# Top-k attention and a gated feed-forward on one core: every step taken from one written list

## The chip, the cores and the metric

The kernel runs on one core of a Trainium2 chip. The metric is the device time of one execution in microseconds (us). The engines of the core work side by side, each through its own queue in order: TensorE (PE, with its weight loads PEld), VectorE (DVE), ScalarE (ACT), GpSimd (POOL), and SyncE (SP), which here issues most DMAs. TensorE writes to PSUM, eight banks of 512 f32 words for each of 128 partitions.

## The reference

Eight batches of eight heads, 576 positions, head width 64; then a feed-forward over 4608 tokens of width 512 with 2048 hidden columns. Its weights come as 64-bit floats.

```python
scores = scale * np.matmul(q, k.transpose(0, 1, 3, 2))
kth = np.partition(scores, -top_k, axis=-1)[..., -top_k:-top_k + 1]   # top_k = 32
scores = np.where(scores >= kth, scores, -1000000000.0)
attn = np.exp(scores - np.max(scores, axis=-1, keepdims=True))
attn = attn / (np.sum(attn, axis=-1, keepdims=True) + 1e-09)
x = heads_side_by_side(np.matmul(attn, v))       # (4608, 512)
h = x @ w_in                                     # w_in (512, 2048)
out = (h * np.cos(h)) @ w_out                    # w_out (2048, 512)
```

## The kernel before

The 4608 tokens are 36 blocks of 128 rows. A *unit* is one block and one pair of heads: 144 units, four to a block; unit n belongs to block n // 4. Each unit goes through these steps:

- `scores`: TensorE multiplies queries by keys into a PSUM tile `sc` (448 columns for each head; two such tiles exist) and into the shared banks `rim` (the last 128). Two units' scores can thus wait at most.
- `take_scores`: ACT copies them to `s` (four buffers).
- `fold_high`, `fold_sum`, `fold_low`: the 576 columns are folded to 288 larger and 288 smaller ones. VectorE makes the larger half (L267, reads `sc` and `s`), POOL the smaller; for units 8 to 10 (`BUSY`) VectorE makes both, the second with `fold_now` (L275). When the last fold that reads `sc` is done, that score tile is free for another unit.
- the search: VectorE finds the 32 largest in rounds of MAX8 and MATCH_REPLACE8: four on the larger halves, two on the smaller.
- `merge_first`, `merge_second`, `distances`, then `mask` and `exponentials` on ACT, `sums` and `reciprocal` on VectorE.
- for units 0 to 3, `turn`: TensorE transposes the probabilities. For all others `split` on POOL (two copies), `write_halves` and `transposes`: two DMAs on SP's queue, out to DRAM and back transposed into `ring` (five places).
- `values`: TensorE multiplies four units' probabilities by v, into `rim`; `take_values`: VectorE scales them into `xT`, the block's input of the feed-forward.

The feed-forward of a block: eight pieces of the first product (`ff1`, here F1.block.piece), two to a PSUM bank `mm` (two banks); `take_first` on ACT empties a bank after every second piece; `reduce_first`, `reduce_second`, `gate` on POOL and `sines` on ACT work on two halves; eight pieces of the second product (`ff2`, here F2.block.piece) gather in one `mm` bank; `take_second` and a DMA bring it out. F2 pieces 0 to 3 need the first gated half, 4 to 7 the second.

The weights arrive as 32 chunks of 512 64-bit columns in staging buffers: `decode_first` (ACT, two instructions), `decode_second` (VectorE, a shift, L151) and `decode_third` (POOL, an addition, L160). Chunks 0 to 15 are `w_in`, 16 to 31 `w_out`.

The order is made by rules: `slot(i, ...)` writes unit i's search and, around it, the later steps of units i-1 and i-2 and the scores of the next one or two units; `feed` puts pieces of F1 and F2 in, by a plan of four slots (`plan`), when `can_first` and `can_second` allow it by counts of ticks; the weight loads go to SP's queue in the first six slots, then to ACT's. Each engine carries out its own share in exactly that order.

Of the kernel before, what the change touches and what calls it, by code (L numbers as in the profile page):

```python
# [30 lines left out]
def kernel(  # L31
# [63 lines left out]
    BUSY = range(8, 11)  # L95
    ff = {"live": 0, "tick": 0, "now": 0, "end": False, "kind": 0, "half": 0, "open": 0, "late": False}

    wq = {"next": 0, "loaded": deque(), "second": deque(), "third": deque(), "done": 0, "ready": 0}

    def staged(spare=0):  # L100
        return sum(c[2] == spare for k in ("loaded", "second", "third") for c in wq[k])

    def load_weights(n, queue):
        for _ in range(n):
            i = wq["next"]
            if i >= len(chunks):
                return
            src, dst = chunks[i]
            if not DECODE:
                queue.dma_start(out=dst[0][:, dst[1]], in_=src)  # L110
                wq["next"] = wq["done"] = i + 1
                continue
            spare = i < 2 * NC + 10 and i % 2 == 1 and staged(1) < XB
            if spare:
                st = ffw.tile([P, CW, 2], I32, tag="x", name="st", bufs=XB)
            elif staged() + ff["live"] >= CHUNKS:
                return
            else:
                st = ffw.tile([P, CW, 2], I32, tag="g", name="st", bufs=CHUNKS)
            queue.dma_start(out=st.rearrange("p w i -> p (w i)"), in_=src)  # L120
            wq["loaded"].append((st, dst, int(spare)))
            wq["next"] = i + 1

# [3 lines left out]
    def decode_first(n):  # L127


        for _ in range(min(n, len(wq["loaded"]))):  # L130
            st, w, spare = wq["loaded"].popleft()
            lo, hi = st[:, :, 0], st[:, :, 1]
            nc.scalar.activation(
                out=w[0][:, w[1]], in_=hi.bitcast(F32), func=AF.Prelu, scale=2.0**-111, alpha=2.0**32
            )
            nc.scalar.mul(out=lo, in_=lo.bitcast(U32), mul=2.0**-29)
            wq["second"].append((st, w, spare))

    def decode_second(n):

        left = min(n, len(wq["second"]))
        while left:
            st, (w, c), spare = wq["second"].popleft()
            wq["third"].append((st, (w, c), spare))
            m = 1
            if left > 1 and wq["second"][0][1][0] is w:
                wq["third"].append(wq["second"].popleft())
                m = 2
            left -= m
            wi = w[:, c : c + m].bitcast(I32)  # L150
            nc.vector.tensor_scalar(  # L151
                out=wi, in0=wi, scalar1=3, scalar2=None, op0=ALU.logical_shift_left
            )

    def decode_third():

        while wq["third"]:
            st, w, _ = wq["third"].pop()
            wi = w[0][:, w[1]].bitcast(I32)
            nc.gpsimd.tensor_tensor(out=wi, in0=wi, in1=st[:, :, 0], op=ALU.add)  # L160
            wq["done"] += 1

# [69 lines left out]
    def scores(u):  # L235
        sc = u["sc"] = ps.tile([P, 2, 512], F32, tag="sc", name="sc", bufs=2)
        for to, k0, k1 in ((sc, 0, SB), (sc_ends[u["n"] % 2], SB, S)):
            for b, q0, rows, r0 in u["parts"]:
                for j in range(2):
                    d = slice(j * D, (j + 1) * D)  # L240
                    st = pairs[b, u["hp"]]
                    nc.tensor.matmul(  # L242
                        to[r0 : r0 + rows, rim_bank(r0, j) if k0 else place(u["hp"], j), 0 : k1 - k0],
                        st["q"][d, q0 : q0 + rows],
                        st["k"][d, k0:k1],
                        start=True,
                        stop=True,
                    )
# [61 lines left out]
    def topk_first(u, w):  # L310

        u["top"] = tops[u["n"] % len(tops)]
        if w:
            merge_first(w)
        if u["n"] not in BUSY:
            fold_sum(u)
        fold_high(u)
        if w:
            merge_second(w)
        if u["n"] in BUSY:  # L320
            fold_now(u)
        topk_round(u, 0, [lambda: distances(w), lambda: None] if w else ())

    def topk_round(u, rnd, between=(), ahead=None):
# [3 lines left out]
        search(  # L328
            at, rest[:, :, HS:S] if rnd == 0 else rest[:, :, 0:HS], rest[:, :, 0:HS], rnd < lasts,
            between if rnd < lasts else (),  # L330
        )
        if rnd < lasts:
            return
        del u["rest"]
        low = u.pop("low")
        for k in range(TOPK // 16):
            more = k < TOPK // 16 - 1
            if ahead and not more:
                ahead()
            search(top[:, :, 1 + 8 * k : 9 + 8 * k, 1], low, low, more, () if more else between)  # L340
# [560 lines left out]
```

## Time and profile before

| what | us |
| --- | --- |
| median of 3 runs | 1412.41 |
| lowest and highest run | 1411.02, 1412.88 |
| time of the profiled execution | 1412.72 |
| span of its trace | 1410.6 |
| granted TensorE clock over the span | 0.975 |

The span runs from the first instruction of the program in the trace to the last; what lies around it is not in the trace. In the page, a line of a group gives the source line, engine, operation, what is written from what, the count, then the busy time and the mean of one in ns, then the idle time of the engine just before them and what ended it. A line of the timeline gives start, duration, engine, line, operation and, in brackets, the wait ahead of it. A line of stretches gives from:to and length, then busy us (and instructions) of PE, PEld, DVE, ACT and POOL, then the granted TensorE clock, the DMA share and GB/s. A line of waits gives the total, how often, and the longest one. TensorE carries out each f32 matmul of the source as two instructions.

### The profile page before, as it was taken

The numbers are of one execution on the slowest core, as the hardware profiler recorded it, in microseconds if no ns is written. First come the engines' busy times: TensorE is split into PE (matmuls) and PEld (weight loads), VectorE is DVE, ScalarE is ACT, GpSimd is POOL, SyncE is SP. The second block draws the span as 40 slices with busy tenths as digits, with TensorE's granted clock in tenths as the row PEclk, the third lists the DMA queues.
The fourth block names the chain that finished last, engine by engine and source line by source line (L and its number), as shares of the span: only waits on it lengthen the run. The fifth ranks groups of instructions, "written<-read, shape, count | busy, mean of one in ns | idle before, by whom it ended". The sixth has DMA issues, their size and how long they took to land.

```text
span 1410.6 us, 32284 instructions
## 1 busy us (share of the span) xinstructions
PE 1354.6 (96%) x11264; PEld 977.2 (69%) x11264; DVE 1336.9 (95%) x5004; ACT 1140.9 (81%) x2043; POOL 1165.3 (83%) x804
## 2 busy tenths in 40 slices
PE   5558999999999999999999999999999999999998
PEld 3445777777777777777777777777777777777775
DVE  7999999999999999999999999999999999999931
ACT  7887888888888888888888888888888888888831
POOL 4778988888888888888888888888888888898810
PEclk6788999999999999999999999999999999999999
DMA  9566776867675576668666576666766566655540
GB/s 291 193 196 181 204 178 169 203 172 196 162 177 152 161 199 159 181 160 197 174 170 159 152 181 187 170 170 160 207 165 165 158 174 166 148 157 146 152 101 15
DMA packets 427442, 240.12 MB, mean 170 GB/s; under 512 B 375952, under 2 KB 392592, under 8 KB 427280
## 3 DMA queue, kind: packets, MB, share of 16 engines
q1 hardware_dynamic: 420720, 224.22, 61.3%
q10 hardware_dynamic: 6560, 13.85, 2.8%
q8 instruction: 88, 1.44, 0.4%
q14 instruction: 74, 0.61, 0.1%
HBM read 45.09 MB, written 101.19 MB: 104 GB/s over the span
## 4 chain that ended last, share of the span: by engine, by line
PE 91%; DVE 7%; ACT 1%; DMA 0%; POOL 0%; issue 0%; SPq 0%; POOLq 0%
PE o L628 36%; PE mm L553 35%; PE rim L475 10%; PE sc L242 8%; DVE top L359 3%; PE rim L242 2%; DVE rest L364 2%; DVE low L364 1%; DVE rest L267 1%; DVE w_out L151 0%; DVE w_in L151 0%; DMA st<-in_moe_w_in_dram 0%; PE warm L844 0%; DVE low L275 0%; ACT s L387 0%; ACT s L378 0%
## 5 line engine op out<-in xcount | busy, mean ns | idle before, releaser
L553 PEld LDWEIGHTS mm<-xT,w_in 128*128 128x128 f32 x4608 | 537.9, 192 | 70.4 <-issue 65.5
L553 PE MATMUL mm<-xT,w_in 128*128 128x128 f32 x4608 | 539.2, 275 | 2.4 <-DVE xT L491 1.7
L628 PE MATMUL o<-w_out,g 128*128 128x512 f32 x1152 | 524.7, 599 | 0.0
L359 DVE MAX8 top<-rest 128x8 f32<-128x288 f32 x1152 | 479.0, 451 | 0.0
L364 DVE MATCH_REPLACE8 rest<-top,rest 128x288 f32<-128x288 f32 x864 | 376.7, 444 | 0.0
L628 PEld LDWEIGHTS o<-w_out,g 128*128 128x128 f32 x1152 | 207.7, 190 | 219.5 <-issue 214.8
L410 POOL COPY halves<-s 128x2304 uint16<-128x2304 uint16 x140 | 294.9, 2107 | 43.3 <-ACT s L387 40.1
L378 ACT ACTIVATE s<-s,top 128x576 f32<-128x576 f32 x288 | 207.6, 768 | 111.1 <-DVE top L352 99.0
L359 DVE MAX8 top<-low 128x8 f32<-128x288 f32 x576 | 241.8, 449 | 0.4 <-POOL low L292 0.4
L387 ACT ACTIVATE s<-s,nd 128x576 f32<-128x576 f32 x288 | 220.4, 769 | 1.1
L292 POOL TENSOR_TENSOR low<-low,rest 128x576 int32<-128x576 int32 x141 | 199.3, 1413 | 11.0
L283 POOL TENSOR_TENSOR low<-s 128x576 int32<-128x576 int32 x141 | 199.6, 1415 | 6.4 <-ACT s L259 6.4
L598 POOL TENSOR_TENSOR x<-g,x 128x1024 f32<-128x1024 f32 x68 | 161.2, 2370 | 5.7
L242 PE MATMUL sc<-k,q 64*64 64x448 f32 (+1 forms) x1120 | 145.6, 564 | 16.2 <-DVE low L275 9.8
L615 POOL TENSOR_TENSOR g<-g,x 128x1024 f32<-128x1024 f32 x68 | 161.0, 2367 | 0.0
L257 ACT COPY s<-rim 64x256 f32<-64x256 f32 (+1 forms) x280 | 103.1, 368 | 61.6 <-PE rim L475 60.0
L475 PE MATMUL rim<-ring,v 128*64 128x128 f32 (+1 forms) x2560 | 139.0, 268 | 0.0
L475 PEld LDWEIGHTS rim<-ring,v 128*64 128x64 f32 x2560 | 130.0, 139 | 6.5 <-issue 5.7
L253 ACT COPY s<-sc 128x896 f32<-128x896 f32 (+1 forms) x144 | 128.4, 892 | 3.3 <-PE sc L242 3.2
L567 ACT ACTIVATE g<-mm 128x512 f32<-128x512 f32 x144 | 85.2, 592 | 56.5 <-PE mm L553 55.5
L364 DVE MATCH_REPLACE8 low<-top,low 128x288 f32<-128x288 f32 x288 | 125.4, 443 | 0.0
L267 DVE TENSOR_TENSOR rest<-sc,s 128x576 f32<-128x576 f32 x144 | 107.7, 748 | 7.1 <-ACT s L259 6.6
(55 smaller groups left out, 1155.7 us busy)
## 6 DMA issues: line engine op xcount, KB each, us to landing
rows<-halves SPq DMA_DIRECT2D x140, 640.0 KB, 3.5
out_dram<-ob ACTq DMA_DIRECT2D x36, 256.0 KB, 2.1
q<-in_q_dram SPq DMA_DIRECT2D x31, 288.0 KB, 4.4
st<-in_moe_w_in_dram SPq DMA_DIRECT2D x16, 512.0 KB, 5.8
v<-in_v_dram SPq DMA_DIRECT2D x32, 256.0 KB, 4.2
k<-in_k_dram SPq DMA_DIRECT2D x31, 144.0 KB, 4.2
k<-in_k_dram SPq DMA_DIRECT2D x32, 128.0 KB, 4.5
st<-in_moe_w_out_dram SPq DMA_DIRECT2D x8, 512.0 KB, 5.1
```

Of the source, the lines that this page charges most:

```text
L242: nc.tensor.matmul(to[r0 : r0 + rows, rim_bank(r0, j) if k0 else place(u["hp"], j), 0 : k1 - k0], st["q"][d, q0 : q0 + rows], st["k"][d, k ...
L283: nc.gpsimd.tensor_tensor(out=u["low"].bitcast(I32), in0=s[:, :, 0:HS], in1=s[:, :, HS:S], op=ALU.add)
L292: nc.gpsimd.tensor_tensor(out=low, in0=low, in1=u["rest"][:, :, HS:S].bitcast(I32), op=ALU.subtract)
L359: nc.vector.max(to[:, j], src[:, j])
L364: nc.vector.match_replace(rest[:, j], to[:, j], src[:, j], NEG)
L378: nc.scalar.activation(out=s[:, j], in_=s[:, j], func=AF.Prelu, bias=less[:, j], scale=1.0, alpha=FAR)
L387: nc.scalar.activation(out=s[:, j], in_=s[:, j], func=AF.Exp, bias=nd[:, j : j + 1], scale=SCALE, accum_out=den[:, j, 0:1],)
L410: nc.gpsimd.tensor_copy(out=halves[:, :, 0 : 2 * S], in_=s.rearrange("p (k h) -> p h k", h=2))
L475: nc.tensor.matmul(to[d, r], lhsT, rhs, start=(bank, j) not in begun, stop=c == NT - 1 and u in us[-2:] and r0 + rows == P,)
L553: nc.tensor.matmul(mm[:, at : at + w], w_in[f // FC][:, c, (f % FC) * P : (f % FC + 1) * P], blk["xT"][:, c], start=c == 0, stop=c == NC - 1,)
L598: nc.gpsimd.tensor_tensor(out=x, in0=g, in1=x, op=ALU.subtract)
L628: nc.tensor.matmul(o, g[:, at : at + P], w_out[f], start=f == 0, stop=f == NF - 1)
```

## The change

The rules (`slot`, `send`, `forward`, `drain`, `feed`, `feed_any`, `can_first`, `can_second`, the queues of pending work) are gone. One list names all steps in order, each by a short name with its unit or block, and a table `steps` maps names to functions; a loop at the end runs them. An engine still carries out its share in the order of the list. Some functions are cut up so that their parts can be listed apart: `scores` into Sa (448 columns) and Sb (the last 128), `turn` into T1, T2, T3 and their copies, `split` into sp1 and sp2, the first search round into R0 (MAX8) and R0m (MATCH_REPLACE8).

What the order does by engine, beside the new names:

- TensorE: the scores of unit 4 stand ahead of unit 0's transposes, those of 8 and 7 ahead of F1.0.0, and so on; from unit 15 on the even unit of a pair comes before the odd one (16, 15, 18, 17, ...), often with F pieces between. F1.0.6 and F1.0.7 come before the scores of unit 10; F2.0.0, F2.0.1 and the values of units 4 to 7 before the scores of unit 12. Ahead of the values of units 8 to 11, 12 to 15 and 16 to 19 there are two more F2 pieces than before, ahead of the next two values one more; from the values of units 28 to 31 on the counts are those of before, and from those of units 132 to 135 on again one to four F2 pieces more.
- VectorE: the shifts of the decode are single ones (before: two chunks in one where they were neighbours) in other places; `take_values` comes after the last MAX8 of a unit in place of before it.
- ACT: single decodes stand between masks, exponentials and score copies; the multiplication of `nd` goes from `mask` to `exponentials`.
- POOL: the same steps with the decode's additions spread.
- SP: all weight loads, those of chunks 24 to 31 too; chunks 0 to 2 are issued before unit 1's queries and keys.

The core of the diff:

```diff
+    def load_weights(k, kind):
+        src, dst = chunks[k]
...
+        nc.sync.dma_start(out=st.rearrange("p w i -> p (w i)"), in_=src)
+        staged[k] = st
...
+    def decode_second(k):
+        w, c = chunks[k][1]
+        wi = w[:, c].bitcast(I32)
+        eng = nc.gpsimd if k in SHIFT_BY_POOL else nc.vector
+        eng.tensor_scalar(
+            out=wi, in0=wi, scalar1=3, scalar2=None, op0=ALU.logical_shift_left
+        )
...
-    def scores(u):
-        sc = u["sc"] = ps.tile([P, 2, 512], F32, tag="sc", name="sc", bufs=2)
-        for to, k0, k1 in ((sc, 0, SB), (sc_ends[u["n"] % 2], SB, S)):
...
+    def scores(u, part):
+        if part == 0:
+            u["sc"] = ps.tile([P, 2, 512], F32, tag="sc", name="sc", bufs=2)
+        to, k0, k1 = ((u["sc"], 0, SB), (sc_ends[u["n"] % 2], SB, S))[part]
...
+    def largest(to, src):
+        late = list(between)
+        between.clear()
         for j in range(2):
             nc.vector.max(to[:, j], src[:, j])
-            if between:
-                between[j]()
...
+            n = (len(late) + 1) // 2
+            for f in late[n * j : n * (j + 1)]:
+                f()
...
-    for i in range(NU):
-        ff["now"] += 1
-        wq["ready"] = wq["done"]
-        u, w, x = (units[i - n] if n <= i else None for n in range(3))
-        z = valued.get(i)
-        slot(i, u, w, x, z)
...
+    for step, *of in order:
+        steps[step](*of)
```

`LOW_BY_POOL` and `SHIFT_BY_POOL` are empty lists, so no decode step changes its engine. `between` holds `distances`, `sums` and `reciprocal` of the unit before until the next MAX8 pair (C in the list puts the last two there).

The list for units 2 and 3 and for units 7 to 16 (Q: load queries and keys; VV: load v; L: load a chunk; D1, D2, D3: decode; K: `take_scores`; P0: merge and folds of VectorE; P0b: `fold_now`; fs, fl: POOL's folds; M: mask; E: exponentials; wr, tr: write and transpose; V, X: `values`, `take_values`; B1, B2: `take_first`, `take_second`; A0, A, N, G: the two reductions, sine and gate):

```
... P0.2 fs.2 L.14.g R0.2 T3e.0 Sa.3 M.1 R0m.2 fl.2 R1.2 Sb.3
D1.7 D1.8 R2.2 E.1 D2.8 R3.2 D3.8 Q0.2 D1.9 T1.1 D1.10 D2.9 T2.1 D2.6 D2.7 K.3 C.1 D3.9 Q1.2
P0.3 ...
B1.0.0 P0.7 B1.0.1 F1.0.4 sp1.5
R0.7 L.28.g M.6 Q.4 R0m.7 Sa.9 R1.7 sp2.5 E.6 fs.7 wr.5 F1.0.5 R2.7 fl.7 D1.28 Sb.9 F1.0.6 D2.25
D1.27 D2.24 R3.7 D3.25 K.9 F1.0.7 Q0.7 D3.24 L.29.g C.6 Q1.7 sp1.6 tr.5 B1.0.2 P0.8 B1.0.3 P0b.8
A0.0.0 M.7 R0.8 Sa.10 Q.5 R0m.8 Sb.10 sp2.6 A.0.0 E.7 R1.8 wr.6 R2.8 D1.29 A0.0.1 K.10 D2.27
D2.26 C.7 D3.27 R3.8 N.0.0 Q0.8 tr.6 sp1.7 Q1.8 P0.9 sp2.7 D3.26 wr.7 P0b.9 M.8 L.30.g R0.9
Sa.11 G.0.0 L.31.g R0m.9 E.8 Sb.11 R1.9 A.0.1 F2.0.0 tr.7 R2.9 K.11 D2.29 D2.28 D1.30 R3.9 D3.29
VV.4 F2.0.1 Q0.9 N.0.1 D3.28 VV.5 C.8 Q1.9 sp1.8 VV.6 P0.10 D1.31 V.4.8 VV.7 P0b.10 M.9 sp2.8
R0.10 G.0.1 wr.8 R0m.10 E.9 R1.10 Sa.12 R2.10 Sb.12 F2.0.2 K.12 sp1.9 tr.8 R3.10 Q0.10 F2.0.3
Q1.10 F2.0.4 X.4.8 fs.11 C.9 P0.11 sp2.9 F1.1.0 wr.9 R0.11 M.10 fl.11 R0m.11 F1.1.1 E.10 R1.11
Sa.13 D2.30 B1.1.0 D2.31 C.10 D3.30 tr.9 Sb.13 R2.11 F2.0.5 K.13 D3.31 R3.11 F1.1.2 Q0.11 sp1.10
F1.1.3 Q1.11 sp2.10 P0.12 fs.12 wr.10 Sa.14 R0.12 M.11 fl.12 R0m.12 Sb.14 F2.0.6 B1.1.1 R1.12
E.11 A0.1.0 F1.1.4 R2.12 tr.10 A.1.0 K.14 F1.1.5 C.11 R3.12 Q0.12 sp1.11 N.1.0 F2.0.7 Q1.12
P0.13 B1.1.2 sp2.11 G.1.0 wr.11 R0.13 Sa.16 M.12 R0m.13 F1.1.6 R1.13 E.12 fs.13 F1.1.7 R2.13
fl.13 tr.11 Sb.16 R3.13 B2.0 sp1.12 B1.1.3 F2.1.0 C.12 Q0.13 O.0 Q.6 K.16 sp2.12 F2.1.1 Q1.13
A0.1.1 wr.12 P0.14 fs.14 Sa.15 R0.14 M.13 R0m.14 fl.14 Sb.15 V.8.12 E.13 R1.14 A.1.1 R2.14 K.15
tr.12 sp1.13 R3.14 F2.1.2 Q0.14 N.1.1 C.13 F2.1.3 Q1.14 sp2.13 wr.13 X.8.12 fs.15 P0.15 F1.2.0
G.1.1 R0.15 M.14 R0m.15 F1.2.1 E.14 R1.15 tr.13 fl.15 Sa.18 R2.15 Sb.18 F2.1.4 B1.2.0 Q.7 R3.15
sp1.14 Q0.15 F1.2.2 K.18 C.14 Q1.15 sp2.14 F1.2.3 wr.14 P0.16 fs.16 R0.16 M.15 Sa.17 fl.16 ...
```

A score tile is taken by the next Sa in the list as soon as the last fold that reads it stands before it; so Sa.16 takes the tile of unit 13, Sa.15 that of unit 14, Sa.18 that of unit 15, Sa.17 that of unit 16.

More of the change, by code (lines that the diff above doesn't have):

```diff
@@ L94 @@
     CHUNKS, XB = 6, 3
[L95 to L122, printed above, removed]
@@ L125 @@
-    UP = 2.0**8 if DECODE else 1.0
[L127 to L153, printed above, removed]
```

826 lines of the change are left out of this document (488 added, 338 removed).

## The prediction

> **What bounds the kernel now.** I read the page first: busy time, slices, chain.
>
> ```profile
> span 1410.6 us, 32284 instructions
> PE 1354.6 (96%) x11264; PEld 977.2 (69%) x11264; DVE 1336.9 (95%) x5004; ACT 1140.9 (81%) x2043; POOL 1165.3 (83%) x804
> PE   5558999999999999999999999999999999999998
> DVE  7999999999999999999999999999999999999931
> PEclk6788999999999999999999999999999999999999
> PE 91%; DVE 7%; ACT 1%; DMA 0%; POOL 0%; issue 0%; SPq 0%; POOLq 0%
> ```
>
> Two engines are full at once: VectorE (DVE) from the second slice to the last but two, TensorE (PE) from the fifth to the end. The stretches and the waits say which of them leads:
>
> ```profile
> 0.00:111.04 111.04, 59.35 (x401) 43.66 (x401) 103.21 (x367) 90.67 (x175) 76.17 (x63) 0.72 0.74 230
> 111.04:133.75 22.71, 22.06 (x177) 16.31 (x177) 20.71 (x79) 17.19 (x31) 17.13 (x13) 0.89 0.57 148
> 133.75:1340.00 1206.25, 1206.25 (x10300) 872.20 (x10300) 1196.70 (x4531) 1012.35 (x1808) 1065.35 (x726) 1.00 0.66 172
> PE rim L436 <- DVE rden L400: 13.7, 4, 4.3
> PE sc L242 <- DVE low L275: 9.8, 3, 4.1
> PE mm L553 <- ACT x L569: 0.7, 1, 0.7
> DVE xT L491 <- ACT s L257: 7.1, 24, 0.8
> DVE xT L499 <- ACT s L257: 3.9, 7, 1.5
> ```
>
> From 133.75 us on TensorE has no idle time at all (1206.25 of 1206.25 us), and VectorE has 9.55 us of it, mostly in short waits for xT, which reads what TensorE's value products leave. So TensorE leads there, and VectorE is only 0.8% behind. Before 111.04 us it is the other way round: TensorE is idle for 51.7 us, because VectorE's search sets the pace. The end is therefore "the last time TensorE had to wait for VectorE, plus all TensorE work queued behind that point". That last real wait stands here, with the waits ahead of it:
>
> ```profile
> 92.85 5.10 PE L553 MATMUL mm<-xT,w_in 128*128 128x128 f32 x32
> ...
> 107.57 0.70 PE L242 MATMUL rim<-k,q 64*64 64x128 f32 x8 [5.70 <-ACT s L257]
> 111.04 1.77 PE L242 MATMUL sc<-k,q 64*64 64x448 f32 x8 [2.76 <-DVE low L275]
> ...
> 112.98 1.10 PE L475 MATMUL rim<-ring,v_tail 64*64 64x128 f32 x16
> 114.02 4.67 PE L475 MATMUL rim<-ring,v 128*64 128x128 f32 x64
> ```
>
> The scores of unit 12 start at 111.04 us, when the second fold of unit 10 frees their score tile. 1410.6 - 111.0 = 1299.6 us follow, of which only one wait of 0.7 us (mm, in the rows of waits) and the last output's way out are not TensorE work.
>
> **What the change removes, adds and moves.** The arithmetic stays: as many matmuls, searches, decodes and copies. Pairs of 512-column shifts become single ones; the DMAs are the same. What moves is order, and with it who waits in whose queue.
>
> *TensorE, units 8 to 16.* Ahead of the scores of unit 12, TensorE now also does F2.0.0, F2.0.1 (the second product's first two pieces of block 0) and the values of units 4 to 7; before they came behind. The values' price is the two rows above: 114.02 + 4.67 - 112.98 = 5.7 us. From here on two score tiles still tie each score to the fold that frees its tile: unit 16's to the fold of unit 13, unit 15's to 14, 18's to 15, 17's to 16. Unit 15's scores tie the tightest. Prices of what lies around them:
>
> ```profile
> 150.06 0.98 PE L242 MATMUL sc<-k,q 64*64 64x448 f32 x8
> ...
> 151.08 0.93 PE L242 MATMUL sc<-k,q 64*64 64x448 f32 x8
> ...
> 156.24 3.70 PE L628 MATMUL o<-w_out,g 128*128 128x512 f32 x8
> 159.77 3.73 PE L553 MATMUL mm<-xT,w_in 128*128 128x128 f32 x32
> ...
> 170.44 0.98 PE L242 MATMUL sc<-k,q 64*64 64x448 f32 x8
> ```
>
> Unit 15's scores begin at 150.06, unit 16's 1.02 us later; two second-product pieces take 159.77 - 156.24 = 3.53 us. Behind 150.06 lie 1410.63 - 150.06 = 1260.6 us. In the new order unit 16's scores and F2.1.0, F2.1.1 have gone ahead: 1260.6 - 1.0 - 3.5 = 1256.0 us remain behind unit 15's scores.
>
> *VectorE up to the fold of unit 14.* These waits stand in its way:
>
> ```profile
> 24.00 0.82 DVE L359 MAX8 top<-low 128x8 f32<-128x288 f32 x2 [0.38 <-POOL low L292]
> ...
> 119.52 0.49 DVE L499 TENSOR_TENSOR xT<-rim,ring 128x128 f32<-128x128 f32 x2 [1.54 <-ACT s L257]
> ...
> 131.38 0.76 DVE L267 TENSOR_TENSOR rest<-sc,s 128x576 f32<-128x576 f32 x1 [0.47 <-ACT s L257]
> ...
> 149.50 0.76 DVE L267 TENSOR_TENSOR rest<-sc,s 128x576 f32<-128x576 f32 x1
> ```
>
> The 0.38 us is POOL's unit-1 fold behind three decode additions; the new list puts the first of them some 6 us earlier. The 1.54 us is xT waiting for values that started behind unit 12's scores; they now start ahead of them, and xT goes after the last MAX8. The 0.47 us is unit 12's score copy, itself behind those values. All three should go: 2.4 us. The work ahead of fold 14 is otherwise equal (all 32 shifts, two xT, fourteen searches), so it ends at 149.50 + 0.76 - 2.39 = 147.9.
>
> *The sum.* 147.9 + 1256.0 = 1403.9 us. The same sum over unit 17 (behind the fold of unit 16, which starts 168.02 in the trace) confirms it:
>
> ```profile
> 168.02 0.75 DVE L267 TENSOR_TENSOR rest<-sc,s 128x576 f32<-128x576 f32 x1
> ```
>
> 168.02 + 0.75 - 2.39 = 166.4; behind unit 17's scores lie 1410.63 - 170.44 = 1240.2, less unit 18's scores (1.0) and F2.1.4 (1.8), now ahead: 1237.4. Together 1403.8.
>
> *Do the values of units 4 to 7 arrive?* They wait for unit 7's transpose on SP's queue:
>
> ```profile
> 101.08 0.34 SPq L441 DMA_DIRECT2D rows<-halves  x1
> 104.23 3.93 SPq L447 DMA_TRANSPOSE ring<-rows  x1
> ...
> ring<-rows SPq DMA_TRANSPOSE x140, 5.1
> st<-in_moe_w_out_dram ACTq DMA_DIRECT2D x8, 512.0 KB, 4.7
> ...
> L160 POOL TENSOR_TENSOR w_out<-w_out,st 128x512 int32<-128x512 int32 x16 | 20.3, 1294 | 16.7 <-ACT s L387 5.2 <-issue 4.5 <-ACT st L136 3.5
> ```
>
> 104.23 + 5.1 = 109.3. Values of 5.7 us end at 115.0; then unit 12's scores with 1299.6 us less values (5.7) and two pieces (3.5) behind them: 115.0 + 1290.4 = 1405.4, less perhaps 2, since that remainder still holds unit 12's scores at a low clock (1.77 us against 0.98) and the 0.7 us wait: 1403.4. This path is as long as the other. Eight weight loads leave ACT's queue for SP's, in front of these writes and transposes; each holds SP until its staging buffer is decoded. The last one ahead of unit 7's transpose waits for one decode addition (1.3 us), which stands on POOL right behind the copies that the write itself awaits; the write then takes 104.23 - 101.08 = 3.2 us to land, so the addition is hidden and I take zero. Without that cover, each us late here is a us at the end.
>
> *New waits.* In unit 2's slot ACT now puts four decodes, two instructions each, between unit 1's mask and unit 3's score copy; before they followed it:
>
> ```profile
> 4.93 1.53 SPq L120 DMA_DIRECT2D st<-in_moe_w_in_dram  x3
> ...
> 33.10 0.88 ACT L253 COPY s<-sc 128x896 f32<-128x896 f32 x1
> 33.89 0.37 ACT L257 COPY s<-rim 128x256 f32<-128x256 f32 x1
> 34.16 0.69 ACT L133 ACTIVATE w_in<-st 128x512 f32<-128x512 f32 x1
> ...
> 35.29 0.67 ACT L133 ACTIVATE w_in<-st 128x512 f32<-128x512 f32 x1
> ...
> 37.81 0.75 DVE L267 TENSOR_TENSOR rest<-sc,s 128x576 f32<-128x576 f32 x1
> ```
>
> One decode costs 35.29 - 34.16 = 1.13 us, four 4.5: the copy would end at 34.3 + 4.5 = 38.8, or at 37.8 if the mask ahead of it starts a us earlier, as fewer decodes stand before that. Unit 3's fold is due at 37.8: a wait of 0 to 1.0 us. I take 0.5, and 0.2 for others of its kind: 1403.9 + 0.7 = 1404.6 us. Unit 1's queries and keys are issued behind three weight loads, 1.5 us later (row at 4.93); their copy stands behind three decodes on ACT anyway, so nothing.
>
> *To the median.* The trace's span is 1410.6, the median of the runs 1412.41: 1.8 us lie around it. 1404.6 + 1.8 = **1406.4 us**, 0.43% faster. Later units keep their order but for single pieces; VectorE's waits for xT there (7.1 us over 24 blocks) shrink, which keeps it as far ahead as the scores need.
>
> [...] In the new order unit 11's scores wait for the second fold of unit 9 after all of block 0's first product: a gap of some 8 us at 92 to 100. [...]
>
> **The rivals.**
> 1. *VectorE's waits only change place.* For it: ACT holds 32 decodes, and an early copy or exponential behind them stalls VectorE at once. Against: ACT is busy 90.67 of 111.04 us. If 2.4 us stay, the sum is 1406.3; with about 6 us of new waits between units 2 and 14 instead of 0.7 it is 1403.9 + 6 + 1.8 = 1411.7: no change.
> [...]
> 3. *The transposes come late on SP's queue* behind weight loads: 1403.4 plus the delay, plus the 1.8 us around the span; it must be over 10 us to be slower. At 12: 1417.2.
> 4. *Nothing moves early*, as two score tiles forbid it: the time stays at 1412.4. The two tiles do hold scores back, but the values and F2 pieces need none.
>
> **How the numbers follow.** Forecast 62% (1403.5 to 1409.5), rival 1 16%, rivals 2 and 3 together 16%, rival 4 3%, more than forecast 3% (1402). A measurement tells about 0.2% (2.8 us) from no change. Faster by more: 62 + 3 = 65%. Within: rivals 1 and 4 = 19%, slower 16%. The range leaves out 3% below and about half of rivals 2 and 3 above, with some of the forecast's tails: 1403 to 1415; the likeliest case alone has 1403.5 to 1409.5.
>
> **What would show it.** Right: TensorE's idle time before 134 us falls from 52 us to about 46, the three VectorE waits above are gone, unit 12's scores start at 113 to 115 us with the values before them, unit 15's just behind the fold of unit 14 at 148 us, and the F pieces of that stretch run at full clock. Wrong: fold 14 later than 149 us, a granted clock below 1 after 130 us, or waits over 3 us at scores.

## The result, and the profile after

The changed kernel takes 1427.97 us (median of 4 runs, 1427.02 to 1429.83); the kernel before, run on the same chip beside it, 1411.91 (4 runs, 1411.02 to 1412.88). The ratio is 1.0115, 95% interval 1.0098 to 1.0133: slower by 16 us, where 6 us faster was forecast. The page of the changed kernel, lines as in the prediction's first fence:

```profile
span 1425.4 us, 32184 instructions
PE 1370.2 (96%) x11264; PEld 970.3 (68%) x11264; DVE 1342.5 (94%) x5017; ACT 1151.3 (81%) x2043; POOL 1168.8 (82%) x804
PEclk6579999999999999999999999999999999999999
PE 77%; DVE 9%; ACT 9%; DMA 2%; SPq 1%; issue 1%; DVEq 0%
```

TensorE counts 15.6 us more of busy time for the same 11264 matmuls: 4.3 of them before 134 us, where the granted clock is lower than before (0.71 against 0.75), and 11.3 behind, where it is 1.00 in both kernels. Short waits can hide in "busy" (the row at 874.41 below comes 0.30 us late and names none); the 11.3 are the first hint that they do. And the chain that ended last, 91% TensorE before, now runs 18% of its way over VectorE and ScalarE. The sums of busy time by stretch, first one stretch of the kernel before, then two of the kernel after. The columns: the stretch and its length, busy time of TensorE, of its weight loads, of VectorE, ScalarE and GpSimd, TensorE's granted clock, the DMA engines' share and GB/s:

```profile
372.80:1218.00 845.20, 845.20 (x7160) 610.93 (x7156) 838.54 (x3174) 708.87 (x1266) 743.96 (x507) 1.00 0.66 171
```

```profile
0.00:111.04 111.04, 63.02 (x403) 46.26 (x404) 103.61 (x362) 92.46 (x177) 78.84 (x63) 0.66 0.75 235
376.40:1230.50 854.10, 852.30 (x7161) 605.91 (x7156) 838.61 (x3174) 715.72 (x1267) 744.41 (x507) 1.00 0.63 169
```

The line of the kernel before and the last line of the kernel after hold the same 23 blocks, from the values of units 32 to 35 to those of 124 to 127: 845.2 us before, 854.1 after, with TensorE idle for at most 1.8 us of them. Setting the two traces side by side by the start of each block's values, the kernel after is 3.0 us late at units 8 to 11 (155.0 against 152.0), 3.6 at units 32 to 35, 12.5 at units 124 to 127, and 14.8 at the end. So there are four places: the early part, blocks 3 to 8, a steady loss of 0.39 us in each later block, and the tail.

What a block pays for is seen when one takes, in TensorE's timeline, the starts of the groups and subtracts them. The kernel before, in one block (ScalarE and TensorE, in order of time; the two L569 and L567 instructions empty the bank of F1 pieces 0 and 1):

```profile
854.66 3.70 PE L628 MATMUL o<-w_out,g 128*128 128x512 f32 x8
854.78 0.75 ACT L257 COPY s<-rim 64x256 f32<-64x256 f32 x2 [1.65 <-PE rim L475]
...
858.20 3.73 PE L553 MATMUL mm<-xT,w_in 128*128 128x128 f32 x32
861.77 3.60 PE L628 MATMUL o<-w_out,g 128*128 128x512 f32 x8
...
863.22 0.68 ACT L569 ACTIVATE x<-mm,quarter 128x512 int32<-128x512 f32 x1
863.79 0.91 ACT L253 COPY s<-sc 128x896 f32<-128x896 f32 x1
...
865.21 3.73 PE L553 MATMUL mm<-xT,w_in 128*128 128x128 f32 x32
```

And the kernel after, at the same place of the same block:

```profile
863.56 3.70 PE L579 MATMUL o<-w_out,g 128*128 128x512 f32 x8
863.68 0.74 ACT L231 COPY s<-rim 64x256 f32<-64x256 f32 x2 [1.16 <-PE rim L477]
864.44 0.91 ACT L227 COPY s<-sc 128x896 f32<-128x896 f32 x1
865.24 0.74 ACT L231 COPY s<-rim 64x256 f32<-64x256 f32 x2
...
867.10 3.73 PE L530 MATMUL mm<-xT,w_in 128*128 128x128 f32 x32
870.67 3.60 PE L579 MATMUL o<-w_out,g 128*128 128x512 f32 x8
...
873.67 0.68 ACT L548 ACTIVATE x<-mm,quarter 128x512 int32<-128x512 f32 x1
...
874.41 3.84 PE L530 MATMUL mm<-xT,w_in 128*128 128x128 f32 x32
```

Before, ScalarE copies one unit's scores behind the values (854.78), and the other unit's only after it has emptied the bank (863.79, behind the row at 863.22). After, both copies come first (863.68, and 864.44 with 865.24), so the bank is emptied 1.6 us later in the block. The two pieces of F1 that need a free bank start 865.21 - 861.77 = 3.44 us after the second pair of F2 before, 874.41 - 870.67 = 3.74 after, right when the bank is empty (873.67 + 0.68 = 874.35). A group that has waited also takes 3.84 us instead of 3.73. 0.30 + 0.11 = 0.41 us; in blocks in which the wait is shorter it is 0.28. The row at 874.41 names no wait, and the rows of waits of the whole trace have 0.2 us of F1 waiting for ScalarE. All other groups of the block have the same start-to-start times in both kernels, in whatever order they stand: the four groups behind the first scores take 14.21 us before (two F2, two F1, two F2, two F1) and 14.21 after (two F1, three F2, two F1, one F2).

### The profile page after: what moved, and what is told of

It is laid out like the page before. It is cut to its first block, busy times and chain, and to the rows that moved or that the text cites. A ratio compares the mean times of both kernels' runs of the same rounds, so it can differ in the third digit from the quotient of the medians.

```text
span 1425.4 us, 32184 instructions
## 1 busy us (share of the span) xinstructions
PE 1370.2 (96%) x11264; PEld 970.3 (68%) x11264; DVE 1342.5 (94%) x5017; ACT 1151.3 (81%) x2043; POOL 1168.8 (82%) x804
## 4 chain that ended last, share of the span: by engine, by line
PE 77%; DVE 9%; ACT 9%; DMA 2%; SPq 1%; issue 1%; DVEq 0%
PE mm L530 31%; PE o L579 27%; PE rim L477 10%; PE sc L216 7%; DVE top L348 4%; PE rim L216 2%; ACT s L376 2%; DVE rest L355 2%; ACT s L367 2%; ACT s L231 1%; ACT L376 1%; DVE rest L241 1%; ACT s L227 1%; ACT g L546 1%; ACT x L548 1%; DVE w_out L131 1%
## 5 line engine op out<-in xcount | busy, mean ns | idle before, releaser
L530 PE MATMUL mm<-xT,w_in 128*128 128x128 f32 x4608 | 546.7, 277 | 3.3 <-DVE xT L499 1.2
L400 POOL COPY halves<-rden 128x256 uint16<-128x256 uint16 x140 | 57.4, 410 | 71.3 <-DVE rden L389 71.3
```

The source lines that it names most:

```text
L530: nc.tensor.matmul(blk["mm"][:, at : at + w], w_in[f // FC][:, c, (f % FC) * P : (f % FC + 1) * P], blk["xT"][:, c], start=c == 0, stop=c ...
```

## The experiments

Each kernel was compared with the kernel before in the same session; medians in us.

### 1. The steady loss: order on ScalarE or on TensorE?

Theory A is the one just read from the rows. Theory B: the new order of scores and pieces on TensorE costs by itself. Theory C: VectorE's xT now stands behind two score copies (VectorE's waits for xT are 19.6 us in the kernel after, 11.0 before), and TensorE waits for xT.

**The even unit's copy behind the bank** (24 blocks; the others alike):

```diff
-... K.96 tr.92 R3.94 F2.21.0 Q0.94 K.95 ... F2.21.3 B1.22.0 R3.95 ...
+... tr.92 R3.94 F2.21.0 Q0.94 K.95 ... F2.21.3 B1.22.0 K.96 R3.95 ...
```

> The changed kernel, but in 24 blocks (scores of units 39 to 132) ScalarE copies the scores of the even unit of the pair before the values (K.40, K.44, ...) only after it has taken the first bank of the next block's first product, not ahead of it; nothing else moves. Theory A, ScalarE's order: two score copies (1.65 us each) stand ahead of the taking of that bank, the third piece of the first product waits for the bank, and TensorE's second pair of the second product takes 3.61 to 3.75 us to the next start instead of 3.44, the piece behind it 3.77 instead of 3.66. With the copy behind it, a block takes 36.70 us again instead of 36.98 to 37.13: 24 blocks by 0.39 us give 9 us, so 1419 us instead of 1428. Theory B, the order of the pieces and of the scores on TensorE itself: no change, 1428. Theory C, VectorE's product xT waits for two score copies instead of one and TensorE waits for xT: xT then waits for one copy, 1419 too; the next run tells A from C.

Measured: 1421.37, 6.6 us less than the changed kernel. In the trace the 23 blocks take 845.9 us (377.66 to 1223.58) instead of 854.1, 8.2 less, of which 1.2 are lost again ahead of them, where the two lists are alike and only one execution differs from another. Its rows:

```profile
866.94 3.60 PE L579 MATMUL o<-w_out,g 128*128 128x512 f32 x8
...
868.39 0.68 ACT L548 ACTIVATE x<-mm,quarter 128x512 int32<-128x512 f32 x1
868.96 0.91 ACT L227 COPY s<-sc 128x896 f32<-128x896 f32 x1
...
870.38 3.73 PE L530 MATMUL mm<-xT,w_in 128*128 128x128 f32 x32
```

3.44 us from one group to the next, and 3.73 for the group, with TensorE's order still the new one. Theory B does not explain this.

**xT ahead of both copies:**

```diff
-... K.96 ... Q0.94 K.95 sp1.93 C.93 F2.21.1 X.88.92 N.21.1 ...
+... Q0.94 sp1.93 C.93 F2.21.1 X.88.92 K.96 K.95 N.21.1 ...
```

> The changed kernel, but in the same 24 blocks the product xT stands ahead of both score copies in the program, so it does not wait for them; ScalarE's own order stays as it is. Theory C: xT no longer waits for ScalarE, the 0.58 us that VectorE waits at it in each block go, and the block takes 36.70 us: 1419. Theory A: VectorE's wait shrinks, but TensorE still waits for the first bank at its third piece: a block stays at 36.98 to 37.13, 1428. Theory B: 1428.

Measured: 1447.57, 19.6 us more. No theory had forecast that. Most of VectorE's wait for xT did go (in its place the folds wait 33.8 us for the copies), and the time rose, because the copies now wait for xT and everything behind them on ScalarE comes later still. Here the wait for the bank is long enough to be named:

```profile
878.39 0.75 ACT L231 COPY s<-rim 64x256 f32<-64x256 f32 x2 [2.28 <-DVE xT L499]
...
884.24 3.60 PE L579 MATMUL o<-w_out,g 128*128 128x512 f32 x8
888.78 3.84 PE L530 MATMUL mm<-xT,w_in 128*128 128x128 f32 x32 [0.94 <-ACT x L548]
```

4.54 us from group to group, and the releaser is L548, the second reader of the bank. Over the 24 blocks these waits come to 20.6 us, about as much as the time rose. This run brings in a wait of its own, so alone it would not decide on theory C. What decides is in the rows above: the first F1 group of a block, which is the one that needs xT, starts 867.10 - 863.56 = 3.54 us after the F2 pair ahead of it in the kernel after, and 858.20 - 854.66 = 3.54 before. TensorE does not wait for xT there, and theory C falls.

**TensorE's old order, ScalarE's new one:**

```diff
-Sa.96 Sb.96 Sa.95 Sb.95   F1.21.4 F1.21.5 F2.20.4 F2.20.5 F2.20.6 F1.21.6 F1.21.7 F2.20.7
+Sa.95 Sb.95 Sa.96 Sb.96   F2.20.4 F2.20.5 F1.21.4 F1.21.5 F2.20.6 F2.20.7 F1.21.6 F1.21.7
```

> The changed kernel, but TensorE's order in the same 24 blocks is that of the kernel before: the odd unit's scores ahead of the even one's, and behind the first pair of scores two pieces of the second product, two of the first, two and two. ScalarE's order stays that of the changed kernel. Theory B: a block takes 36.70 us, 1419. Theories A and C: the waits before the third piece stay and so does the block's time, 1428 (within 2).

Measured: 1467.34. The wait at the bank is unchanged, as A says; the rest is a wait that this mixture made itself, since ScalarE now copies the even scores first while TensorE makes them last, and the last scores stand behind a fold (35.5 us in 26 waits):

```profile
894.60 3.60 PE L579 MATMUL o<-w_out,g 128*128 128x512 f32 x8
898.34 3.84 PE L530 MATMUL mm<-xT,w_in 128*128 128x128 f32 x32
...
921.05 0.98 PE L216 MATMUL sc<-k,q 64*64 64x448 f32 x8 [1.44 <-DVE rest L241]
```

898.34 - 894.60 = 3.74 with the old order of pieces. The total of this run says nothing for or against B.

**The counterpart: the old order, whole, as a list, and then with only the copy ahead.** First the control, in which the list holds the order of the kernel before. Of the change it keeps that each shift stands alone, and also, which the expectation does not say, that all weight loads are on SP's queue and that `nd` is multiplied in `exponentials`:

> The order of the kernel before, whole, written as a list for the changed kernel's functions; the only thing of the change that is left in it is that each weight piece is shifted by itself, where before 13 instructions shift two pieces at once. Theory D2: 26 shifts of 0.42 us for 13 of 0.68 us cost VectorE 2.1 us by unit 14, and the end comes up to 2 us later than before: 1412 to 1415. Rival, it is not the order that costs but how the program is made up: 1420 or more.

Measured: 1413.57, ratio 1.0008 (0.9999 to 1.0018). Then with one edit in 24 blocks:

```diff
-... K.95 ... B1.22.0 K.96 ...
+... K.95 K.96 ... B1.22.0 ...
```

> The counterpart of the later copy: the order of the kernel before as a list (1413.6), but in 24 blocks ScalarE copies the scores of the even unit right behind those of the odd one, ahead of the next block's first bank, as the changed kernel does; TensorE's order is the old one. Theory A: a block takes 0.3 to 0.45 us longer (36.70 to 37.0 to 37.15), the second pair of the second product 3.6 to 3.75 instead of 3.44: 1420 to 1424. Rival (theory B): TensorE's order is the old one, so no change: 1413.6.

Measured: 1423.20, 9.6 us more than the control, ratio to the kernel before 1.0082 (1.0066 to 1.0097). The 23 blocks take 853.4 us (373.34 to 1226.70), 8.1 more than in the kernel before; the pair of F2 takes 3.62 to 3.76 us to the next group, and some of the waits, about 0.15 us each, are named as L548's. Theory A is shown from both sides.

### 2. The tail

The run with the later copy, and from the fold of unit 130 on the old order:

> The run with the later copy (1421.4), and from the fold of unit 130 on the order of the kernel before. Theory: of the 2.2 us that this run still loses between the values of units 124 to 127 and the end, single scores and single pieces of the second product on TensorE and a fold that waits 2.7 us for its scores are the cause, and they go: 1419. Rival, that loss is only the early part's, drawn along: 1421.

Measured: 1417.76, 3.6 us less than with the later copy alone. VectorE's wait of 2.7 us at the fold of unit 141 goes, and from the values of units 124 to 127 to the end of the last matmul TensorE takes 188.9 us instead of 190.7. So the order of the tail costs 1.8 us. The other 1.8 by which the medians differ cannot come from the edit: the medians are of two sessions, and at units 32 to 35, far ahead of the tail, where the lists are alike, the two profiles stand 1.4 us apart already. What the tail's 1.8 are made of was not tried one by one; it has more single scores and single pieces, whose price the next section shows.

### 3. Blocks 3 to 8 and the early part

Single scores stand between pieces in blocks 3 to 8 of the kernel after. Their price, in block 4:

```profile
200.34 3.73 PE L530 MATMUL mm<-xT,w_in 128*128 128x128 f32 x32
204.01 0.98 PE L216 MATMUL sc<-k,q 64*64 64x448 f32 x8
...
205.14 1.98 PE L579 MATMUL o<-w_out,g 128*128 128x512 f32 x4
206.96 3.73 PE L530 MATMUL mm<-xT,w_in 128*128 128x128 f32 x32
```

One unit's scores alone take 205.14 - 204.01 = 1.13 us, a pair 2.10; the single piece behind them 1.82, half of a pair of F2 1.72. Each change between scores and pieces thus costs some 0.1 us, and a block with four single scores has up to eight more of them. The sum can be read from the two traces: from the values of units 8 to 11 to those of 32 to 35 the kernel after has two pieces of F2 less to do (184 matmuls against 192, 3.5 us), because they were done ahead, and it still takes 0.6 us more, 221.4 against 220.8, in 81 groups instead of 66. So the small steps cost about 4 us there, some 0.5 of it waits at the bank, and eat up what the early part had done ahead.

**The new order up to the fold of unit 14, the old order behind it:**

> The changed order up to the fold of unit 14, and behind it the order of the kernel before (steps that were done early are left out of it). Theory A with E (the loss lies in ScalarE's order in each later block, 0.39 us, and in the single scores of blocks 3 to 8, each 1.13 us where a pair takes 2.10, with 0.09 more in the pieces beside them): from the values of units 12 to 15 on every block takes 36.70 us. The values of units 8 to 11 start 3.0 us later than before (155.0 against 152.0), but two pieces of the second product (3.4 us) and one unit's scores (1.0 us) more are done by then. If TensorE's work alone sets the end: 1410.6 + 3.0 - 4.4 = 1409.2 of span, 1411 of time. If VectorE's lateness (fold of unit 14 at 153.0 against 149.5) sets the values: 1414 of span, 1416 of time. Rival, the early part is what costs: 1421 or more.

Measured: 1415.68, ratio 1.0024 (1.0015 to 1.0033): 2.1 us less than the run with the later copy and the old tail (the traces: from the values of units 8 to 11 to those of 32 to 35 it takes 220.3 us against 222.5). What is left to the kernel before lies ahead of the fold of unit 14, which comes at 152.06 us against 149.50. Two pieces of F2, 3.5 us of TensorE's work, are done earlier than before; the unit's scores that the expectation adds are not, since by the start of the values of units 8 to 11 both kernels have made equally many. Even so the values of units 12 to 15 start 36.2 us after those of 8 to 11, where the kernel before needs 36.7: TensorE waits 2.0 us for xT there and 0.6 for the bank. In this run the work that went ahead is paid back as waiting.

**Shifts clear of GpSimd, first try:**

```diff
-P0b.8 A0.0.0 ... R2.8 D1.29 A0.0.1 K.10 D2.27 D2.26 C.7 ...
+P0b.8 D2.27 D2.26 A0.0.0 ... R2.8 D1.29 A0.0.1 K.10 C.7 ...
```

> The changed kernel, but the decode shifts of weight pieces 27 and 26 (2.32 and 1.26 us at 97.08 and 99.32, while GpSimd is inside a 2.36 us subtraction and the instruction behind it) stand right behind the second fold of unit 8, where GpSimd waits for a transfer; nothing else moves. Theory D, shifts that meet a long GpSimd instruction are held up: both take 0.42 us there, VectorE folds unit 9 at 101.2 us instead of 103.9, the values of units 8 to 11 start at 152.4 instead of 155.0, and the end comes 2.6 us earlier: 1425.4. Rival, TensorE's own backlog or its lower clock in the first 155 us sets the values' start: unchanged, 155.0 and 1428.

Measured: 1427.86, no change. The two shifts still met GpSimd's instructions there (1.19 and 1.26 us), so it tests theory D only in part: the fold of unit 10 was 1.1 us earlier, and by unit 23 nothing of it was left.

**All colliding shifts cleared, on the old order behind unit 14, and then with nine pairs joined:**

> As the run with the old order behind unit 14 (1415.7, fold of unit 14 at 152.1), and the shifts of weight pieces 3 and 5, 6 and 7, 26 and 27, 28 and 29, 30 and 31 are put where GpSimd is between two instructions, with its additions behind both shifts of a pair; each is still shifted by itself. Theory D: the shifts that took 1.0, 1.5, 2.3, 1.3, 0.9 and 1.0 us instead of 0.42 (5.5 us more in all in the changed kernel) lose most of that: VectorE folds unit 14 at 148 to 149, and since VectorE sets the values there, the end comes 2 to 3.5 us earlier: 1412 to 1413.5. Rival, something else holds VectorE there, its scores or ScalarE's decode: fold of unit 14 stays at 151 to 152 and the time at 1415.7.

> As the run with the shifts put clear of GpSimd, and nine neighbouring pairs of them (1 and 2, 6 and 7, 10 and 11, 17 and 18, 21 and 22, 24 and 25, 26 and 27, 28 and 29, 30 and 31) are one instruction each, as before. Theory D2: 0.68 us for a pair in place of two by 0.42 but starting 0.33 apart (0.75 from the first's start to the second's end) gives 0.1 to 0.16 us each, 1 us in all: 1 us earlier than without the pairs, 1411 to 1412.5, level with the kernel before. Rival: no difference from the run without pairs.

Measured: 1415.07 and 1415.27, against 1415.68: no difference that can be told. The shifts that were moved did get short (0.41 to 0.43 us each but one, 0.82), but VectorE's time went into a wait at xT. It is named as one for ScalarE's copy of unit 12's scores, and these stand on TensorE behind the values of units 4 to 7:

```profile
100.79 0.74 DVE L131 TENSOR_SCALAR w_out<-w_out 128x512 int32<-128x512 int32 x2
...
122.59 0.49 DVE L492 TENSOR_TENSOR xT<-rim,ring 128x128 f32<-128x128 f32 x2 [1.12 <-ACT s L231]
```

The fold of unit 9 came at 101.6, that of unit 14 at 151.8 us. (Profiles of one order differ by up to 1 us here, as unit 0's fold starts between 6.6 and 7.8.) The run does not isolate theory D, though: two additions (2.54 us) now stand together on GpSimd ahead of the first `gate`, which starts 1.5 us later than without the edit (106.82 against 105.33), F2.0.0 waits for it until 109.22 instead of 107.74, and the values of units 4 to 7 start at 115.66 instead of 112.83. What short shifts alone would give is not shown; this way of clearing them gains nothing.

A harder version, pairs behind the third round of each unit with the additions in reverse order, went wrong in its own way:

> As the run with the old order behind unit 14, and in the first eleven units the shifts are made in pairs again, right behind the third round of a unit, with GpSimd's additions behind them in reverse order (so that the additions do not start between the shifts), and behind the subtraction of that unit. Theory D, the early shifts cost VectorE what the early scores gained: VectorE spends 12 instead of 18.5 us on shifts, the fold of unit 14 comes at 147 to 149 us instead of 153.0, and the end is 3 to 4 us earlier than without the pairs: some 1408, below the kernel before. Rival, the transposes or TensorE's backlog set the values: the same as without the pairs, within 1 us.

Measured: 1426.19. With the additions put later a piece of F1 waited 11.2 us, named as a wait for GpSimd's addition to `w_out`; that this comes of staging buffers kept full, which share their tiles with the feed-forward's `g`, is the likely reading and was not tried. It tells nothing on D.

**What holds the values of units 4 to 7.** One timeline of the kernel after, four engines in order of time:

```profile
83.61 0.39 POOL L400 COPY halves<-rden 128x256 uint16<-128x256 uint16 x1
84.75 0.43 SPq L172 DMA_DIRECT2D q<-in_q_dram  x1
...
86.72 0.58 SPq L179 DMA_DIRECT2D k<-in_k_dram  x1
87.35 0.57 SPq L443 DMA_DIRECT2D rows<-halves  x1
...
93.33 2.10 POOL L394 COPY halves<-s 128x2304 uint16<-128x2304 uint16 x1 [3.31 <-DMA rows<-halves]
...
96.75 2.36 POOL L564 TENSOR_TENSOR x<-g,x 128x1024 f32<-128x1024 f32 x1
97.08 3.50 DVE L131 TENSOR_SCALAR w_out<-w_out 128x512 int32<-128x512 int32 x2
...
105.55 1.77 PE L216 MATMUL sc<-k,q 64*64 64x448 f32 x8 [11.82 <-DVE low L249]
...
108.45 6.17 PE L579 MATMUL o<-w_out,g 128*128 128x512 f32 x8 [0.71 <-POOL g L573]
...
108.91 3.45 SPq L449 DMA_TRANSPOSE ring<-rows  x1
...
114.56 0.67 PE L477 MATMUL rim<-ring,v_tail 64*64 64x128 f32 x16
```

Unit 5's halves are complete at 84.0, but their write stands on SP's queue behind the loads of q and k of Q.4 and is issued at 87.35. The halves have one buffer, so GpSimd's split of unit 6 waits for that write (3.31 us), and everything behind it on GpSimd is late: its subtraction starts at 96.75 and meets the shifts, which take 3.50 us instead of 0.74, the rows of units 6 and 7, and unit 7's transpose, issued at 108.91 where it was 104.23 before. Four runs, on the old order behind unit 14:

**The loads back at their old places on SP's queue:**

```diff
-... M.6 Q.4 R0m.7 ... Sa.10 Q.5 R0m.8 ... VV.4 F2.0.1 ... VV.7 ...
+... wr.9 Q.4 ... wr.10 Q.5 ... wr.12 VV.4 ... wr.14 VV.5 ... wr.16 VV.6 ... wr.17 VV.7 ...
```

> As the run with the old order behind unit 14 (1415.7), and on SP's queue the loads of q and k of units 16 to 23 (Q.4, Q.5) and of the second batch's v (VV.4 to VV.7) stand where the kernel before has them, behind the written rows of units 9, 10, 12, 14, 16 and 17. Theory F, those loads hold up the rows: unit 5's halves were done at 84.0 us but their write was issued at 87.35, and GpSimd's next split waited 3.3 us for it. Without them the transpose of unit 7 is issued at 104 to 106 us instead of 108.3 and the values of units 4 to 7 start at 110 to 111 instead of 112.8; the end comes 1 to 2 us earlier, 1414 to 1415. Rival: TensorE's two pieces or VectorE's folds hold them: the values stay at 112.8 and the time at 1415.7.

Measured: 1413.15, 2.5 us less; ratio to the kernel before 1.0008 (0.9998 to 1.0017).

```profile
85.15 0.34 SPq L443 DMA_DIRECT2D rows<-halves  x1
...
91.18 2.10 POOL L394 COPY halves<-s 128x2304 uint16<-128x2304 uint16 x1
...
94.60 2.36 POOL L564 TENSOR_TENSOR x<-g,x 128x1024 f32<-128x1024 f32 x1
...
106.10 5.28 PE L579 MATMUL o<-w_out,g 128*128 128x512 f32 x8
106.14 3.34 SPq L449 DMA_TRANSPOSE ring<-rows  x1
...
111.31 0.67 PE L477 MATMUL rim<-ring,v_tail 64*64 64x128 f32 x16
```

The write follows the halves, the split waits no more, unit 7's transpose is issued 2.8 us earlier and the values start 3.3 us earlier than in the kernel after; against the run that this one edits they start 1.5 us earlier (111.31, 112.83). GpSimd's subtraction is over before the shifts come: the sixteen shifts of `w_out` take 6.1 us instead of 10.1 in the kernel after and 8.9 in the run edited, although none was moved. So theory F holds, and the long shifts of `w_out` were for the most part its consequence.

**The other three** (the first two pieces of F2 behind the values; the loads and the cleared shifts; all three):

> As the run with the old order behind unit 14, and the first two pieces of the second product, which stand ahead of the values of units 4 to 7 on TensorE, stand behind them. Theory G: they wait for GpSimd's gate until 108.4 us and run 6.2 us there at the halved clock; without them the values start as soon as the last transpose has landed, at 111 to 113, and VectorE gets its product xT earlier by as much. Alone that gives under 1 us, since the transpose lands at about 112 to 113: 1415 to 1416. Rival: these pieces were done while TensorE waited anyway, and behind the values they cost 3.6 us: 1417 to 1419.

> The cleared shifts (1415.1) and the old places of the loads on SP's queue together. Theories D and F together: VectorE no longer waits 1.1 us for xT, and the fold of unit 14 comes at 149.5 to 150.5; 1412 to 1413.5. If TensorE's two pieces hold the values (theory G): the values of units 4 to 7 stay at 114 to 116 and the time at 1414 to 1415.

> Cleared shifts, old places of the loads on SP's queue, and the two pieces behind the values. If D, F and G all hold: the values of units 4 to 7 start at 109 to 111, VectorE folds unit 14 at 148 to 149.5, no later than the kernel before, and the end comes at 1409.5 to 1412 of time, at or below the kernel before. If the early part is set by VectorE's own work up to unit 9 (folds 1.5 to 2 us later than before there already): the fold of unit 14 at 151 to 152, 1414 to 1415.

Measured: 1418.41, 1413.30 and 1416.25. With the pieces behind the values these start earlier, at 110.7 and 109.2, but wait for unit 7's rows and run at a low clock themselves (0.52 and 0.66 between 111 and 118 us), so they end at 120.0 and 117.8, against 118.0 and 118.7 without that edit. The time rises by 2.7 and 3.0 us: the pieces, 5.2 and 6.4 us long there against 3.60 at a granted clock of 1.00, had stood in a gap of TensorE and filled it. Theory G falls. Clearing the shifts adds nothing to the loads, with the same later gate as above (105.66 against 103.69).

### 4. Do the parts add up, and can the kernel before be beaten?

> The changed kernel with three things undone at once: the second copy on ScalarE is behind the first bank in 24 blocks, the tail from the fold of unit 130 on is the old one, and the loads of q, k of units 16 to 23 and of the second batch's v stand at their old places on SP's queue. Blocks 3 to 8 and all else of the early part stay as the change has them. If the parts add up: 1417.8 - 2.5 = 1415.3. If the loads cost only beside the old order behind unit 14: 1417.8.

Measured: 1415.96, 1.8 us less than 1417.76, which the same kernel took with the loads ahead of the rows. Of the 2.5 expected, most is there, though the two 95% intervals (1.0016 to 1.0033, 1.0026 to 1.0049) overlap.

> The run with the loads at their old places (1413.2) and nine neighbouring pairs of shifts as one instruction each. Theory D2 in its weak form: VectorE's fold of unit 14 comes 0.5 to 1 us earlier than 150.3 and, since TensorE is full from the values of units 12 to 15 on and these wait for VectorE, the end comes up to 1 us earlier: 1412.2 to 1413, level with the kernel before. Rival: no difference, 1413.2.

Measured: 1411.95, ratio to the kernel before 0.9996 (0.9987 to 1.0005): the fold of unit 14 comes at 149.1 us, and no difference to the kernel before is left. No version that was run is faster than the kernel before. Undone one after the other:

| what is undone, on top of the line above | median | less |
| --- | --- | --- |
| the changed kernel | 1427.97 | |
| second copy ahead of the bank (24 blocks) | 1421.37 | 6.6 |
| order of the tail from unit 130 on (1.8 of it in the tail) | 1417.76 | 3.6 |
| order from unit 14 on (blocks 3 to 8 above all) | 1415.68 | 2.1 |
| loads ahead of the rows on SP's queue | 1413.15 | 2.5 |
| shifts one by one | 1411.95 | 1.2 |

The rows are medians of different sessions, and the 95% interval of a ratio to the kernel before is about 0.1% wide to each side, 1.4 us. The 6.6 us stand well clear of that. The 2.5 us do so barely, and have the trace and the repeat above for them; the 3.6 and 2.1 rest on the stretches of the traces; the last row is not shown to differ from nothing. The control with the old order and single shifts lies as far from the kernel before (1413.57 against 1412.39), but its interval holds 1 as well, and it also has the loads on SP's queue.

## Why the prediction was wrong

**The step that failed most** is the last sentence of the sum: "Later units keep their order but for single pieces". It was costed at nothing. But the order had also changed on ScalarE, by one score copy per block, from behind the bank to ahead of it, which the section on the change does not name either. VectorE's waits for xT, which the same sentence has shrinking, grew from 11.0 to 19.6 us by it, and cost nothing that TensorE's rows show; the two pieces that need the bank had 865.21 - 863.90 = 1.3 us of slack (863.90 is the end of the row at 863.22), and the bank came 1.6 us later. 24 edits give 6.6 us (undone) to 9.6 (made alone); in the traces' 23 blocks it is 8.2 and 8.1. The "single pieces" of that sentence were not free either: about 4 us in blocks 3 to 8, as much as had been done ahead. With that sentence falls "1256.0 us remain behind unit 15's scores": this was taken from the kernel before, where TensorE has no waits, and in the kernel after 1425.4 - 153.8 = 1271.6 us lie behind the fold of unit 14.

**VectorE's fold of unit 14** was put at 147.9 and ended at 153.0 + 0.75 = 153.8. The three waits went, as forecast: behind unit 0's fold VectorE waits 0.9 us for two decodes there, and for no copy, no xT and not for GpSimd. But the shifts, costed as equal, took 18.5 us instead of 12.4. That accounts for the delay: 6.1 us of shifts, less the three waits (2.4), plus the new ones (0.9), and unit 0's fold 1.1 earlier, make 3.5 us, and 153.0 - 149.5 is 3.5. About 1 us of the 6.1 is single shifts in place of pairs (thirty-two short ones took 13.4 us in the run with the cleared shifts); the rest is shifts that were held up.

**"The addition is hidden and I take zero"**, for SP's queue: the weight loads were looked at, and the loads of q and k were not. They had been moved from behind the rows of units 9 and 10 to ahead of those of 5 and 6, which the section on the change leaves out. Unit 7's transpose, forecast to land at 109.3, was issued at 108.91. Rival 3 named this place with another load, and needed a delay of over 10 us for a slower kernel; it was 4.7 us there, and about 2.5 at the end.

**The new waits** on ScalarE in unit 2's slot did not appear: VectorE had no wait at the fold of unit 3. Unit 1's later loads let TensorE wait 7.6 us for its keys, but VectorE folds unit 1 at 16.8 us, against 17.2 before, so they cost nothing that was seen.

**The clock**: the forecast gap before unit 11's scores is there (11.82 us, forecast some 8). The granted clock is 1.00 from 94.0 to 96.3 us, inside that gap, and 0.50 from 97 to 113 us; the two F2 pieces behind the gap take 6.17 us against 3.60 at a granted clock of 1.00. The values, which the sum had at 5.7 us, took 4.2, with a granted clock of 1.00 from 114.5 to 118.8 us. From 133.75 us on the granted clock is 1.00 in both kernels: the time there was not lost to the clock.

**Rival 1**, VectorE's waits changing place, comes nearest up to unit 14, but the time came back as shifts that GpSimd held up, and not as stalls behind ScalarE's decodes. No rival had the end at 1428, since each took TensorE behind unit 15 as full and equal.

**What it would show**: TensorE's idle time before 134 us fell to 48.0 us (from 52, forecast 46), but unit 12's scores start at 118.8 us (forecast 113 to 115) and unit 15's at 154.0 (forecast 148); "fold 14 later than 149 us" was named as the sign that it is wrong, and came true.

## What to carry to other kernels

A step that moves is a step in every queue that it passes: list for each engine what now stands behind it, and ask for each of those who waits. An engine that is full on both sides of a change still has slack at single places; the slack in front of a PSUM bank here was 1.3 us, and 1.65 us of copy went into it. When a trace shows no waits and the busy time has grown, subtract the starts of the groups in one period of both kernels: the group that has become longer names the place.

## What the runs showed of the hardware

- A short wait hides in TensorE's busy time. In the kernel after F1's groups came 0.17 to 0.31 us late in each of 24 blocks, and the rows of waits show 0.2 us of it in all; only from about 0.3 us late is a wait named, and then about 0.16 us short (0.15 us named where the group came 0.31 late, 0.94 where it came 1.10 late). After such a wait the group of 32 takes 3.84 us instead of 3.73.
- A VectorE shift of 128x512 int32 takes 0.42 us. Started 0.33 us into a 2.36 us subtraction of GpSimd it took 2.32 us, and ended 0.29 us after that; MATCH_REPLACE8 kept its 0.44 us and two MAX8 their 0.81 inside another subtraction of the kernel after (2.37 us from 176.23 on). Of the three only the shift was held up; why, no run here shows.
- Changing between scores and pieces costs TensorE about 0.1 us each time (one unit's scores alone 1.13 us, a pair 2.10), which small steps spread over a full engine pay again and again: with 81 groups in place of 66 some 3.5 us, beside 0.5 of waits.
